# Two A/B transformer layers, forward and backward, on one core: gradient rows kept in SBUF, inner gradients turned through two small tiles, slope loads a group ahead

## The chip, the cores and the metric

The kernel runs on one core of one Trainium2 chip. It is written in Bass with the Tile framework: the program names tiles in pools, and the framework places them in SBUF or PSUM, orders each engine's instructions by a planner of its own and sets every semaphore. The metric is the device time of one execution in microseconds (us); lower is better.

## The reference

`x` has 2048 rows of D = 512, all in bf16. Four layers follow one another, A, B, A, B, each with a LayerNorm and a residual, and both A layers share their weights, as do both B layers. The kernel returns the output and, for a given `grad_out`, the gradients of `x` and of the five weights.

```python
def _A_ref(x, wqkv, wo):                       # linear attention, 32 heads of 16
    q, k, v = split(x @ wqkv)
    phi = lambda t: jnp.where(t > 0, t + 1, jnp.exp(t)) + 1e-6
    kv = einsum("bhsd,bhse->bhde", phi(k), v); z = phi(k).sum(over s)
    o = (phi(q) @ kv) / (phi(q) . z + 1e-6)
    return merge_heads(o) @ wo
def _B_ref(x, w_gate, w_up, w_down):           # GLU, F = 1376
    return (sigmoid(x @ w_gate) * (x @ w_up)) @ w_down
x = x + _A_ref(ln(x)); x = x + _B_ref(ln(x)); x = x + _A_ref(ln(x)); x = x + _B_ref(ln(x))
_out, _vjp = jax.vjp(_f, A_x, A_wqkv, A_wo, B_w_gate, B_w_up, B_w_down)
_grads = _vjp(grad_out)
```

The listing is shortened; `ln` is the LayerNorm without scale and shift.

## The kernel before

**Tiling.** A row tile is 128 rows; a block is four of them (512 rows), so there are four blocks. F is cut into eleven chunks of 128 (`NFC`), the last of which overlaps the one before it by 32 columns (`FDUP`). A step is one chunk `fc` of one block `b`.

**Stages.** The forward layers 0, 1 and 2 come first. The last GLU, layer 3, does forward and backward together (`b_both`): in each step `glu` makes the gate and up products of a chunk, four matmuls multiply `grad_out` turned (`gT3_t`) with the turned down weight (`wdT`), and `scale` multiplies the result into the pair of slopes, which gives the inner gradient `dd` of the chunk (in the tile `sd_t`). At step 1 or 2 of the next block, `down(b - 1)` makes the output rows and `dh_b(b - 1)` multiplies the inner gradients with the turned up and gate weights `wuT` and `wgT`, row tile by row tile, eleven matmuls each; `ln_bwd` then takes each row tile through the LayerNorm and adds the gradient rows (`gn_t`). Behind that come the backward of layer 2 (`a_bwd`), of layer 1 (`b_bwd`), of layer 0, and the weight gradients (`dw_cols`, `dw_rows`, `dw_small`).

**The fill.** The down weight's gradient of layer 3 (`Fill`, 176 matmuls) has no consumer before the end. It is given out in small portions between the matmuls of the backward layers. Its operands are the hidden rows, read turned from DRAM (`hf_t`), and the gradient rows (`gf_t`), which it loads itself, into the same pool as `hf_t`.

**Inner gradients in DRAM.** The weight gradients need `dd` with rows on the partitions. Block 0 is stored as it is and turned when it is read. Blocks 1 to 3 are turned on the spot: `turn_dd` turns each chunk with one DMA into a tile `nat_t` that collects four chunks (1024 KB), and when a set of columns is full, the tile is queued in `k.nats` and a later `flush_nat` stores it. Chunk 10 overlaps chunk 9 in that tile, so chunk 9 is turned after it.

**Queues.** SP issues the loads, the turning DMAs and most stores, POOL (`k.st`) the others. An instruction of a queue that waits holds up all behind it. The framework's planner decides the order; a DMA that is not ready in its plan is passed by others that are.

**Buffers.** `h_t` and `hT_t` have four buffers each and serve LayerNorm rows, gradient rows and their turned copies in all stages. `wuT` and `wgT` are allocated from the right end of SBUF when layer 2 has left it, and loaded turned at once (`load_b_bwd`, L438 and L439). PSUM has eight banks; in the forward stages `bank` takes them alternately from two tags of four.

**Slopes.** `b_bwd` reads the slopes of layer 1 in groups of three or four chunks into `sh_t`, two buffers, at the start of each group (L937, L938).

Of the kernel before, what the change touches and what calls it, by code (L numbers as in the profile page):

```python
# [16 lines left out]
D = 512  # L17
# [38 lines left out]
class K:  # L56
    spread_banks, n_bank = True, 0
# [13 lines left out]
def kernel(  # L71
# [72 lines left out]
    k.wb = ExitStack()  # L144
# [82 lines left out]
class Fill:  # L227


    def __init__(self, k):  # L230
        self.k, self.sv = k, k.sv[3]
        self.g = [k.p_set.tile([P, NB, D], BF16, name="gf_t", tag="set_t") for _ in range(NBLK)]
        for b in range(NBLK):
            k.nc.sync.dma_start(out=self.g[b][:], in_=by_tile(k.g_in, b * NB, NB))
        self.todo = self.run()
# [115 lines left out]
def forward(k):  # L351
    nc, tc = k.nc, k.tc
    with ExitStack() as ctx:
# [29 lines left out]
        for b, fc in b_both(k, 3, lns[3], ctx):  # L383
            if b == 0:
# [5 lines left out]
                if next(second, None) is None and actx:  # L390
                    flush_turned(k)
                    actx.close()
                    wb = w_pool(k, "wb")
                    k.wuT = wb.tile([P, NFC, D], BF16, name="wuT")
                    k.wgT = wb.tile([P, NFC, D], BF16, name="wgT")
                    load_b_bwd(k, k.wuT, "wu", k.last_mul)
                    load_b_bwd(k, k.wgT, "wg", k.last_mul)
                    actx = None
# [318 lines left out]
def last_grads(k, b):  # L717

    k.gns[b] = k.p_h.tile([P, NB, D], BF16, name="gn_t", tag="h_t")
    k.nc.sync.dma_start(out=k.gns[b][:], in_=by_tile(k.g_in, b * NB, NB))  # L720
    k.gTs[b] = k.p_hT.tile([P, NDC, SB], BF16, name="gT3_t", tag="hT_t")
    k.nc.sync.dma_start_transpose(out=k.gTs[b][:], in_=k.g_in[rows(b * NB, NB), :])


def b_both(k, l, ln, ctx):
# [4 lines left out]
    k.n_t, k.fused, k.early = 2, lambda st: True, []  # L730

    def down(b):
        for j in range(NB):
# [3 lines left out]
            if j % 2 == 0:  # L737
                ost = k.p_o.tile([P, 2, D], BF16, name="o0_t")
            nc.vector.tensor_tensor(ost[:, j % 2, :], y_ps[:], k.xs[st][:], ALU.add)
            if j % 2:  # L740
                k.st.dma_start(out=by_tile(k.out0, st - 1, 2), in_=ost[:])

    def scale(b, fc, dhh, dd):
        k.last_mul = nc.vector.tensor_tensor(dd, dhh[:].unsqueeze(1).to_broadcast([P, 2, SB]), dd, ALU.mult)  # L744
        if b:
            if fc == NFC - 2:
                return
            turn_dd(k, sv, b, fc, dd)
            if fc == NFC - 1:
                turn_dd(k, sv, b, fc - 1, dds[b][fc - 1])  # L750
# [4 lines left out]
    for b in range(NBLK):  # L755
        ln.need(b * NB + NB - 1)
        hhs[b], dds[b] = [], []
        if b == 1:
            k.p_ln, k.p_o, k.p_nat, k.p_wt = pool("ln3", 2), pool("o3", 2), pool("nat", 2), pool("wt", 1)
        for fc in range(NFC):  # L760
# [18 lines left out]
            if b in (1, 2) and fc in (6, 8, 10):  # L779
                turn_weight(k, fc // 2 - 3 + 3 * (b - 1))  # L780
            if b == 2 and fc == 5:
# [7 lines left out]
    flush_nat(k, k.st)  # L789
# [12 lines left out]
def turn_dd(k, sv, b, fc, dd):  # L802

    i, f = divmod(fc, 4)
    p0 = FDUP if fc == NFC - 1 else 0
    if f == 0:
        k.nat = k.p_nat.tile([P, 2, NB, D], BF16, name="nat_t")
    k.nc.sync.dma_start_transpose(
        out=k.nat[:, :, :, f * P - p0:(f + 1) * P - p0].rearrange("p a j f -> p (a j) f"),
        in_=dd.rearrange("p a s -> p (a s)"))  # L810
    if f == 1:
        flush_nat(k)
    if f == 3 or fc == NFC - 2:
        w = SETS[i][1]
        k.nats.append((sv["ddN"][b, i, :, :, :, 0:w], k.nat[:, :, :, 0:w]))
# [13 lines left out]
def dh_b(k, l, b, dds, h, up=None):  # L829
    for j in range(NB):  # L830
        st = b * NB + j
        dh_ps = k.bank([P, D], F32, name="dh_ps")
        for i in range(2 * NFC):
            a, fc = divmod(i, NFC)
            k.nc.tensor.matmul(dh_ps[:], lhsT=dds[fc][:, a, rows(j)], rhs=(k.wuT, k.wgT)[a][:, fc, :],  # L835
                               start=(i == 0), stop=(i == 2 * NFC - 1))
        ln_bwd(k, l, st, dh_ps[:], h[:, j, :], k.xs[st][:] if up is None else up[:, j, :])
# [5 lines left out]
def backward(k):  # L843
    nc, tc = k.nc, k.tc
    with ExitStack() as ctx:
        pool = lambda name, bufs, **kw: ctx.enter_context(tc.tile_pool(name=name, bufs=bufs, **kw))
        k.spread_banks = False
        mctx = ctx.enter_context(ExitStack())
        mpool = lambda name, bufs: mctx.enter_context(tc.tile_pool(name=name, bufs=bufs))
        k.p_set, k.p_sh = mpool("dw_set", 6), mpool("sh", 2)  # L850
# [11 lines left out]
        k.p_all = pool("dw_all", 2, side="right")  # L862
        a_bwd(k, 0, True)
        k.fill.step(NFC * NST)
        h3, h1 = (load_all(k, sv[l]["h"], k.p_all, "all", k.marks[b]) for l, b in ((3, 2), (1, 3)))
        joint = lambda i, a: dw_cols(k, ("wu", "wg")[a], 0, SETS[i],
                                     [(h3, sv[3]["ddT"][a], sv[3]["ddN"][:, :, :, a]), (h1, sv[1]["ddT"][a])])
        k.p_dst, k.n_put = mpool("dw_stage", 6), 0
# [3 lines left out]
        k.p_set = pool("dw_set_end", 12)  # L872
# [16 lines left out]
def ln_bwd(k, l, st, dh_ps, h_st, up):  # L889
# [9 lines left out]
    junk = k.p_ln.tile([P, D], BF16, name="junk", bufs=1)  # L899
    nc.vector.scalar_tensor_tensor(junk[:], t_sb[:], -1.0 / D, h_st, ALU.mult, ALU.mult, accum_out=c2[:])  # L900
# [8 lines left out]
def b_bwd(k, l):  # L909
    nc, sv = k.nc, k.sv[l]  # L910
    with ExitStack() as ctx:
# [21 lines left out]

        gTs[0], k.early = k.early, []
        for b in range(NBLK):
            for f0, nf in FGRP:
                sh = k.p_sh.tile([P, 4, 2, SB], BF16, name="sh_t", tag="sh")  # L937
                nc.sync.dma_start(out=sh[:, 0:nf].rearrange("p f a s -> p f (a s)"),  # L938
                                  in_=sv["sd"][:, b * NFC + f0:b * NFC + f0 + nf])
                for fc in range(f0, f0 + nf):  # L940
                    i = fc - f0
                    ps = k.bank([P, SB], F32, name="dhh_ps")
# [244 lines left out]
def dw_small(k):  # L1187
# [3 lines left out]
    for l in (2, 0):  # L1191
        sv = k.sv[l]
        C = k.p_set.tile([P, NDC, D], BF16, name="C_l", tag="set_t")
        nc.sync.dma_start_transpose(out=C[:], in_=sv["CT"][:])
        ET = k.p_set.tile([P, NDC, D], BF16, name="ET_l", tag="set_t")
# [19 lines left out]
def load_all(k, src, pool, tag, first=None):  # L1215
# [4 lines left out]
    else:  # L1220
        ts = [pool.tile([P, NB, D], BF16, name="rows_t", tag=tag)[:] for _ in range(NBLK)]
# [6 lines left out]

def pieces(k, nat, src, c0, w, turned=None):

    for b in range(NBLK):
        t = k.p_set.tile([P, NB, w], BF16, name="set_t", tag="set_t")
# [81 lines left out]
```

## Time and profile before

| What | Value |
|---|---|
| Median of 7 runs | 1109.94 us (1107.54 to 1113.09) |
| The profiled execution, its own time | 1111.71 us |
| Its span, first to last instruction | 1110.0 us |
| Granted TensorE clock | 0.996 |
| Busy time: PE, DVE, ACT, POOL | 1068.1, 552.3, 445.1, 301.1 us |
| DMA traffic | 260.07 MB, mean 234 GB/s |
| `nat_t<-sd_t` turning DMAs | 33, 4.1 us to landing |
| `sv_ddN<-nat_t` stores | 6 of 1024 KB and 3 of 704 KB |
| `gn_t` and `gf_t` loads | 4 and 4 of 512 KB |

How to read it: PE is TensorE's matmuls, PEld its weight loads, DVE VectorE, ACT ScalarE, POOL GpSimd, SP SyncE. A row of the groups names line, engine, operation, output and inputs, then busy time and mean duration, then the idle time before it and who ended it. Matmuls overlap in time, so a matmul's listed duration (379 ns) is longer than the distance to the next. The time of the profiled execution includes 1.7 us around its span.

### The profile page before, as it was taken

Reading aid. Unit: us, or ns where it says so; the run is one execution under the profiler, and the core shown is the slowest. Engines: PE = TensorE matmul, PEld = TensorE weight load, DVE = VectorE, ACT = ScalarE, POOL = GpSimd, SP = SyncE. Lnnn points to the kernel's source line nnn. Section 1 sums busy time; section 2 is a strip of 40 time slices with the busy share of each in tenths; the row PEclk is TensorE's granted clock in tenths of the full one; section 3 lists DMA queues with packets and bytes.
Section 4 is the critical chain, followed back from the end, with each engine's and each line's share of the span. In section 5 each row is a group of like instructions: output and inputs, shape, how many; then the busy total and the mean of one; then the engine's idle time right before and its main releaser. Section 6 shows DMA issues by size and latency. Waiting matters only on the chain.

```text
span 1110.0 us, 15238 instructions
## 1 busy us (share of the span) xinstructions
PE 1068.1 (96%) x5448; PEld 495.9 (45%) x5448; DVE 552.3 (50%) x1029; ACT 445.1 (40%) x930; POOL 301.1 (27%) x403
## 2 busy tenths in 40 slices
PE   6989899999989999999899999999999999999998
PEld 3444344444434444444344444443444444465443
DVE  7686865668834445444667535556876200001110
ACT  3476766548634646363234534433235200000010
POOL 5333534204631616141532200002623100011120
PEclk9999999999999999999999999999999999999999
DMA  8997977789994979899997897868989899599990
GB/s 249 257 254 246 282 213 231 217 196 230 301 212 106 268 183 266 212 248 264 319 333 211 222 282 226 237 190 232 350 235 339 225 248 203 123 212 229 258 233 29
DMA packets 387741, 260.07 MB, mean 234 GB/s; under 512 B 305424, under 2 KB 356400, under 8 KB 385616
## 3 DMA queue, kind: packets, MB, share of 16 engines
q1 hardware_dynamic: 372416, 208.98, 75.0%
q0 software_dynamic: 15248, 50.11, 13.6%
q8 instruction: 43, 0.70, 0.3%
q14 instruction: 34, 0.28, 0.1%
HBM read 77.76 MB, written 106.79 MB: 166 GB/s over the span
## 4 chain that ended last, share of the span: by engine, by line
PE 55%; DMA 2%; DVE 2%; ACT 2%; issue 1%; POOL 1%; SPq 0%; ACTq 0%; POOLq 0%; DVEq 0%
PE dw_ps L1258 18%; PE dh_ps L926 6%; PE dh_ps L1103 4%; PE dhh_ps L196 4%; PE dh_ps L835 3%; PE dw_ps L1276 3%; PE dh_ps L1094 2%; PE CT_ps L1022 2%; PE fill_ps L252 2%; PE y_ps L196 2%; PE dpk_ps L196 2%; PE dq_ps L196 2%; PE g_ps L196 1%; PE u_ps L196 1%; DMA qn_l<-sv_qn 1%
## 5 line engine op out<-in xcount | busy, mean ns | idle before, releaser
L1258 PE MATMUL dw_ps<-set_t,rows_t 128*128 128x512 bf16 (+1 forms) x1024 | 204.4, 362 | 0.0
L1258 PEld LDWEIGHTS <-rows_t 128*128 128x128 bf16 x1024 | 100.2, 98 | 103.6
L666 POOL TENSOR_TENSOR sd_t<-sd_t,hh_t 128x512 bf16<-128x512 bf16 x68 | 81.4, 1197 | 165.4 <-DVE hh_t L661 83.7
L1183 DVE CAST dw_new<-dw_ps 128x512 bf16<-128x512 f32 (+1 forms) x20 | 12.4, 654 | 185.4 <-PE dw_ps L1258 185.0
L1183 ACT CAST dw_new<-dw_ps 128x512 bf16<-128x512 f32 (+1 forms) x20 | 10.5, 561 | 225.7 <-PE dw_ps L1258 188.1
L896 ACT ACTIVATE t_sb<-dh_ps,rstd 128x512 f32<-128x512 f32 x64 | 43.5, 680 | 141.9 <-PE dh_ps L835 102.4
L196 PE MATMUL dhh_ps<-gT_t,wdT 128*128 128x512 bf16 x352 | 90.5, 379 | 1.8 <-ACT dhh_t L945 1.8
L196 PE MATMUL g_ps<-hT_t,wg 128*128 128x512 bf16 (+1 forms) x360 | 90.7, 374 | 1.3 <-DVE sd_t L663 0.6
L196 PE MATMUL u_ps<-hT_t,wu 128*128 128x512 bf16 (+1 forms) x360 | 90.7, 374 | 0.5 <-DVE hh_t L661 0.2
L926 PE MATMUL dh_ps<-wuT,dd_t 128*128 128x512 bf16 x176 | 66.7, 379 | 0.0
L926 PE MATMUL dh_ps<-wgT,dd_t 128*128 128x512 bf16 x176 | 66.7, 379 | 0.0
L661 DVE SCALAR_TENSOR_TENSOR hh_t<-sd_t,u_ps 128x512 bf16<-128x512 bf16 x88 | 59.4, 679 | 5.8 <-ACT sd_t L660 5.0
L660 ACT ACTIVATE sd_t<-g_ps,onef 128x512 bf16<-128x512 f32 x88 | 60.1, 691 | 2.5
L1184 POOL DMA_DIRECT2D out_dram<-dw_new x36 | 19.3, 541 | 154.2 <-DVE dw_new L1183 92.0
L947 DVE TENSOR_TENSOR dd_t<-dhh_t,sh_t 128x1024 bf16<-128x1024 bf16 x44 | 30.0, 691 | 59.9 <-ACT dhh_t L945 49.9
L835 PEld LDWEIGHTS <-sd_t 128*128 128x128 bf16 x352 | 34.8, 99 | 48.8 <-issue 8.7
L659 ACT ACTIVATE g_ps<-g_ps 128x512 f32<-128x512 f32 x88 | 52.4, 600 | 7.8 <-PE g_ps L196 7.4
L744 DVE TENSOR_TENSOR sd_t<-dhh_t,sd_t 128x1024 bf16<-128x1024 bf16 x44 | 30.4, 690 | 49.9 <-POOL sd_t L666 48.5
L196 PEld LDWEIGHTS <-wdT 128*128 128x128 bf16 x352 | 34.4, 98 | 43.5 <-issue 2.6
L196 PEld LDWEIGHTS <-wu 128*128 128x128 bf16 x360 | 35.2, 98 | 41.5 <-issue 0.7
L196 PEld LDWEIGHTS <-wg 128*128 128x128 bf16 x360 | 34.5, 98 | 42.0 <-issue 2.7
L926 PEld LDWEIGHTS <-dd_t 128*128 128x128 bf16 x352 | 34.4, 98 | 41.5
(166 smaller groups left out, 1841.9 us busy)
## 6 DMA issues: line engine op xcount, KB each, us to landing
sv_sd<-sd_t SPq DMA_DIRECT2D x22, 512.0 KB, 3.8
sv_ddT<-dd_t SPq DMA_DIRECT2D x40, 256.0 KB, 4.6
sv_h<-h_t POOLq DMA_DIRECT2D x16, 512.0 KB, 5.9
sv_qr<-pe_t POOLq DMA_DIRECT2D x16, 512.0 KB, 4.9
sh_t<-sv_sd SPq DMA_DIRECT2D x8, 1024.0 KB, 7.0
rows_t<-sv_h SPq DMA_DIRECT2D x16, 512.0 KB, 7.2
sv_ddN<-nat_t SPq DMA_DIRECT2D x6, 1024.0 KB, 6.0
set_t<-sv_ddN SPq DMA_DIRECT2D x12, 512.0 KB, 6.5
```

Source lines behind the costliest of these rows:

```text
L196: i = k.nc.tensor.matmul(out, lhsT=lhs(c), rhs=rhs(c), start=(c == 0), stop=(c == n - 1))
L659: nc.scalar.activation(g_ps[:], g_ps[:], ACT.Tanh, scale=-0.5)
L660: nc.scalar.activation(sd[:, 0, :], g_ps[:], ACT.Identity, bias=k.onef[:], scale=-1.0)
L661: nc.vector.scalar_tensor_tensor(hh[:], sd[:, 0, :], 0.5, u_ps[:], ALU.mult, ALU.mult)
L666: nc.gpsimd.tensor_tensor(sd[:, 1, :], sd[:, 1, :], hh[:], ALU.mult)
L744: k.last_mul = nc.vector.tensor_tensor(dd, dhh[:].unsqueeze(1).to_broadcast([P, 2, SB]), dd, ALU.mult)
L835: k.nc.tensor.matmul(dh_ps[:], lhsT=dds[fc][:, a, rows(j)], rhs=(k.wuT, k.wgT)[a][:, fc, :], start=(i == 0), stop=(i == 2 * NFC - 1))
L896: nc.scalar.activation(t_sb[:], dh_ps, ACT.Identity, scale=rstd, accum_out=c1[:])
L926: nc.tensor.matmul(acc[b][j][:], lhsT=dd[:, a, rows(j)], rhs=(k.wuT, k.wgT)[a][:, fc, :], start=(fc == 0 and a == 0), stop=(fc == NFC - 1 ...
L1103: nc.tensor.matmul(dh[j][:], lhsT=lhs(j, c), rhs=rhs(c), start=False, stop=stop and c == NDC - 1)
L1258: k.nc.tensor.matmul(ps[ic][:, 0:w], lhsT=h_m[:, ic * P:(ic + 1) * P], rhs=t_m, start=(m == 0), stop=(m == n - 1))
L1276: k.nc.tensor.matmul(p[0:r, :], lhsT=t[:, f:f + r], rhs=g_t, start=(i == 0 and st == 0), stop=(i == len(srcs) - 1 and st == NST - 1))
```

## The change

- The gradient rows of blocks 1 to 3 are loaded in their own block, at step 4, into a pool `gf` on the right side that lives to the end of the kernel; the fill uses them there. Those of block 0 still come early into `h_t` for `ln_bwd`, and once more at the end of `b_both` into the one-buffer pool `g0`, for the fill. At the end the hidden rows of layer 1 (`h1`) take these buffers.
- `turn_dd` collects two chunks instead of four, in a tile of 512 KB, alternately from a pool of its own and from `g0`, before that holds gradient rows. Every call first flushes what is queued. Chunk 10 has a tile of its own. The last flush goes to SP, not to POOL.
- `dh_b` of block 0 takes the four row tiles through `wuT` first and then through `wgT`, in four banks.
- `ln_bwd` in `b_both` writes an unused product to the PSUM bank it has read instead of to SBUF. `down` stores single row tiles.
- `b_bwd` loads each group of slopes one group ahead.
- In the tail, the pools for pieces, stages and rows are cut and placed anew: `dw_set` has two buffers and a right-side pool four, in turn.

```diff
@@ Fill
-        self.g = [k.p_set.tile([P, NB, D], BF16, name="gf_t", tag="set_t") for _ in range(NBLK)]
-        for b in range(NBLK):
-            k.nc.sync.dma_start(out=self.g[b][:], in_=by_tile(k.g_in, b * NB, NB))
+        self.g = k.gf
@@ forward, when layer 2 has left SBUF
+                    k.p_gf, k.p_g0 = gpool("gf", NBLK - 1), gpool("g0", 1)
                     wb = w_pool(k, "wb")
@@ last_grads
-    k.gns[b] = k.p_h.tile([P, NB, D], BF16, name="gn_t", tag="h_t")
-    k.nc.sync.dma_start(out=k.gns[b][:], in_=by_tile(k.g_in, b * NB, NB))
+    if b == 0:
+        k.gns[b] = k.p_h.tile([P, NB, D], BF16, name="gn_t", tag="h_t")
+        k.nc.sync.dma_start(out=k.gns[b][:], in_=by_tile(k.g_in, b * NB, NB))
...
+def rows_kept(k, b):
+    t = (k.p_gf if b else k.p_g0).tile([P, NB, D], BF16, name="gf_t", tag="gf_t")
+    k.nc.sync.dma_start(out=t[:], in_=by_tile(k.g_in, b * NB, NB))
+    return t
@@ b_both, down
-            if j % 2 == 0:
-                ost = k.p_o.tile([P, 2, D], BF16, name="o0_t")
-            nc.vector.tensor_tensor(ost[:, j % 2, :], y_ps[:], k.xs[st][:], ALU.add)
-            if j % 2:
-                k.st.dma_start(out=by_tile(k.out0, st - 1, 2), in_=ost[:])
+            ost = k.p_o.tile([P, D], BF16, name="o0_t")
+            nc.vector.tensor_tensor(ost[:], y_ps[:], k.xs[st][:], ALU.add)
+            k.st.dma_start(out=k.out0[rows(st), :], in_=ost[:])
@@ b_both, scale, loop and end
         if b:
-            if fc == NFC - 2:
-                return
             turn_dd(k, sv, b, fc, dd)
-            if fc == NFC - 1:
-                turn_dd(k, sv, b, fc - 1, dds[b][fc - 1])
...
+            if b and fc == 4:
+                gns[b] = rows_kept(k, b)
...
-    flush_nat(k, k.st)
+    flush_nat(k)
+    k.gf = [rows_kept(k, 0)] + [gns[b] for b in range(1, NBLK)]
     dh_b(k, l, b, dds[b], ln.h[b], gns[b])
@@ turn_dd
-    if f == 0:
-        k.nat = k.p_nat.tile([P, 2, NB, D], BF16, name="nat_t")
+    if f % 2 == 0:
+        k.n_nat = 1 - k.n_nat
+        k.nat = (k.p_g0, k.p_nat)[k.n_nat].tile([P, 2, NB, 2 * P], BF16, name="nat_t", tag=("gf_t", "nat_t")[k.n_nat])
...
-    if f == 1:
-        flush_nat(k)
-    if f == 3 or fc == NFC - 2:
-        w = SETS[i][1]
-        k.nats.append((sv["ddN"][b, i, :, :, :, 0:w], k.nat[:, :, :, 0:w]))
+    flush_nat(k)
+    if f % 2 or fc == NFC - 1:
+        p0, p1 = (0, 2 * P) if f % 2 else (FDUP, P)
+        c0 = f // 2 * 2 * P
+        k.nats.append((sv["ddN"][b, i, :, :, :, c0:c0 + p1 - p0], k.nat[:, :, :, p0:p1]))
@@ dh_b
+    dh = {}
+    for a, j in [(a, j) for a in range(2) for j in range(NB)] if b == 0 else [(a, j) for j in range(NB) for a in range(2)]:
+        if a == 0:
+            dh[j] = k.bank([P, D], F32, name="dh_ps")
+        for fc in range(NFC):
+            k.nc.tensor.matmul(dh[j][:], lhsT=dds[fc][:, a, rows(j)], rhs=(k.wuT, k.wgT)[a][:, fc, :],
+                               start=(a == fc == 0), stop=(a == 1 and fc == NFC - 1))
+        if a:
+            ln_bwd(k, l, b * NB + j, dh[j][:], h[:, j, :], up[:, j, :])
@@ ln_bwd
-    junk = k.p_ln.tile([P, D], BF16, name="junk", bufs=1)
+    junk = dh_ps if k.scrap_ps else k.p_ln.tile([P, D], BF16, name="junk", bufs=1)[:]
@@ b_bwd
+        groups = [(b, f0, nf) for b in range(NBLK) for f0, nf in FGRP]
+        shs = [slopes(*groups[0])]
...
+                sh = shs[-1]
                 for fc in range(f0, f0 + nf):
                     i = fc - f0
+                    if i == 1 and len(shs) < len(groups):
+                        shs.append(slopes(*groups[len(shs)]))
@@ backward, pools
-        k.p_set, k.p_sh = mpool("dw_set", 6), mpool("sh", 2)
+        k.p_set, k.p_sh = mpool("dw_set", 2), mpool("sh", 2)
...
-        k.p_all = pool("dw_all", 2, side="right")
+        k.p_all, p_first = pool("dw_all", 1, side="right"), pool("dw_first", 4, side="right")
...
+        h3 = load_all(k, sv[3]["h"], k.p_all, "all", k.marks[2])
+        h1 = load_all(k, sv[1]["h"], k.p_gf, "gf_t", k.marks[3])
+        k.set_pools = [p_first] * 4 + [k.p_set] * 2
...
-        k.p_dst, k.n_put = mpool("dw_stage", 6), 0
+        k.p_dst, k.n_put, k.n_set = pool("dw_stage", 6, side="right"), 0, -1
```

## The prediction

> **What bounds the kernel now.** I read the windows by stage first, because a mean over the whole span says nothing about the stage that an edit touches; then the waits of TensorE (PE), then the order of time around the two places that the diff moves.
>
> ```profile
> 337.00:490.00 153.00, 152.69 (x706) 68.89 (x705) 73.79 (x123) 89.11 (x180) 59.19 (x73) 1.00 0.86 209
> 515.50:545.00 29.50, 26.29 (x122) 11.65 (x120) 17.77 (x38) 12.20 (x24) 12.04 (x12) 1.00 1.00 262
> 630.00:755.00 125.00, 123.20 (x570) 55.63 (x569) 58.15 (x102) 48.17 (x107) 4.95 (x5) 1.00 0.80 225
> 860.00:1105.00 245.00, 245.00 (x1240) 120.20 (x1238) 26.16 (x43) 15.76 (x34) 29.57 (x51) 1.00 0.87 198
> ```
>
> First number after the stretch is its length, second PE's busy time. In the last GLU after its first block (337 to 490) PE misses 0.3 us, in the weight gradients (from 860) nothing. An edit there can only lose. What is left is in holes, and the waits name them:
>
> ```profile
> PE dh_ps L835 <- DMA wgT<-in_B_w_gate_dram: 4.2, 1, 4.2
> PE CT_ps L1022 <- DMA qn_l<-sv_qn: 2.7, 1, 2.7
> PE dhh_ps L196 <- ACT dhh_t L945: 1.8, 3, 1.0
> PE dh_ps L835 <- DMA wuT<-in_B_w_up_dram: 1.5, 1, 1.5
> ```
>
> The largest belongs to `dh_b` of block 0. In PE's order of time:
>
> ```profile
> 326.41 2.53 PE L835 MATMUL dh_ps<-wuT,sd_t 128*128 128x512 bf16 x11 [1.48 <-DMA wuT<-in_B_w_up_dram]
> 333.10 4.11 PE L835 MATMUL dh_ps<-wgT,sd_t 128*128 128x512 bf16 x11 [4.15 <-DMA wgT<-in_B_w_gate_dram]
> 337.00 2.69 PE L835 MATMUL dh_ps<-wuT,sd_t 128*128 128x512 bf16 x11
> 339.53 2.54 PE L835 MATMUL dh_ps<-wgT,sd_t 128*128 128x512 bf16 x11
> ```
>
> Eleven matmuls start 2.37 us apart as a group (339.53 to 341.90). PE does the eleven of wuT, then stands 4.15 us until wgT is there, and the eleven after it take 3.90 us (333.10 to 337.00) instead of 2.37: after the stop PE runs at half pace for a while. The DMA queue of SP says why wgT is late:
>
> ```profile
> 312.53 9.30 SPq L438 DMA_TRANSPOSE wuT<-in_B_w_up_dram  x1
> 321.88 1.27 SPq L439 DMA_TRANSPOSE wuT<-in_B_w_up_dram  x1
> 323.21 5.98 SPq L438 DMA_TRANSPOSE wgT<-in_B_w_gate_dram  x1
> 329.23 1.26 SPq L439 DMA_TRANSPOSE wgT<-in_B_w_gate_dram  x1
> ```
>
> The four transposes go out one behind the other; the last lands 4.1 us after 329.23, at 333.3.
>
> **Part 1: `dh_b` of block 0 goes by weight, not by row tile.** All four row tiles do wuT first. From 326.41 that is 44 matmuls, 4 x 2.37 = 9.5 us, so wgT is wanted at 335.9 instead of 328.8, and it is there at 333.3: 2.6 us to spare. Gone are the wait (4.15) and the half pace (3.90 - 2.37 = 1.5, and 0.15 in the next group): **-5.8 us**. The wait for wuT (1.48) stays; next after that nothing is late, as the GLU behind it has its inputs. The four `ln_bwd` now end 2.37 us apart; on DVE each costs 0.69 + 0.75 + 0.75 = 2.2 us, so DVE just keeps up and is at most about 1 us late for the next GLU, which PE runs ahead of by its banks. If wgT landed 2.6 us later than now, the gain would begin to shrink. Its new place in SBUF (16 KB lower, over the query tiles of layer 2) makes it wait for the stores of those; the last sv_qr store is issued at 299 and such stores take 4.9 us, and the sv_qn store for which wuT waits today ends later, at 312.5. So no delay.
>
> Of the two rules on the stop: the trace shows half pace after 4.15 us of waiting, and also after 2.40 us at 763.75, but not after 2.70 us at 543. The Trainium skill, "TensorE: Matmul & The Clock Gate", What's actually happening, puts the fall to half clock after an idle window of about 3.4 us. By the rule a new stop under 3.4 us would cost only itself, by the row at 763 it can cost 1.6 more; I price rivals by the row.
>
> **Part 2: gradient rows.** Loads of 512 KB fall from eight (gn x4, gf x4) to five. The three that go are 0.4 to 1.2 us of SP's queue each, between 490 and 502, where nothing waits for them: 0 on the path. The block's row load at fc 4 of its own block is wanted by `dh_b` more than 20 us later and lands in 5.0 to 6.5: hidden. The tag h_t loses three users, so the copies of `a_grads` 2, which today start at 517.88 when the h tile of block 3 frees, can go earlier, and their two transposes leave SP before 519. That takes some 4 us of SP work from ahead of the qn_l load whose lateness costs 2.7 us at 543. Between 0 and -2.7; I take 0, since SP's order there is the scheduler's and hf_t (6.0 us of SP) stays in front of it.
>
> **Part 3: two small tiles for the turned gradients.** The 33 transposes stay (4.1 us to land). The nine stores become 18: of 512 KB where they were 1024, in runs of 512 bytes. SP gets about 9 x 0.5 us more issue over 180 us. The waits are new. Each tile is refilled two pairs later: two transposes 2.6 us apart, 4.1 to land, the store 3.2 to 6.0 to land (wT 512 KB 3.2, the 1024 KB store 6.0), the issues 2: 12 to 15 us, against 4 x 2.59 = 10.4 us in which PE makes four more. So SP falls behind by 2 to 5 us per two pairs, and what is queued behind a blocked transpose waits too: weight turns and their stores (now written out at the next step, behind their own 8 us transpose), the transposes gT, hT, gaT. Against that stand margins: hT of block 2 lands about 7 us before PE asks, gT more, and each block has 28 us of `down` and `dh_b` in which SP catches up. The inner gradient tiles sd_t have a ring of 14 steps. Cost on the path in blocks 1 and 2: 0.
>
> In the last block there is no such gap. A rule speaks against the change here: the Trainium skill, "DMA: Bandwidth & Descriptors", Rules for kernel authors, wants 1 MiB or more per DMA, and its fit (Anatomy of one DMA[...]) is about 2.0 us fixed plus bytes over 436 GB/s: 3.2 us for half a store where the whole took 4.4. The trace's rows are 3.2 to 6.0 us. At the end the chain is: transpose of fc 10 waits for its tile, lands, its store lands, then the gradient rows of block 0 load into the same buffer, and the fill's first matmul needs them. SP today:
>
> ```profile
> 489.87 0.60 SPq L821 DMA_DIRECT2D sv_ddN<-nat_t  x1
> 499.93 1.23 SPq L808 DMA_TRANSPOSE nat_t<-sd_t  x1
> 501.97 3.14 SPq L240 DMA_TRANSPOSE hf_t<-sv_hhT  x1
> 505.48 0.34 SPq L1000 DMA_DIRECT2D MT_l<-wT  x1
> 507.10 5.75 SPq L240 DMA_TRANSPOSE hf_t<-sv_hhT  x1
> ```
>
> Stepping through the pairs of block 3 with 4 us per transpose and 5.5 per store I get the transpose of fc 10 at 499, landed 504, stored 509, rows there at 514. Today's fill starts at 515.35. By the page's 3.2 us it would be 507. If hf_t and MT_l are queued behind the row load, hf_t lands at 516.5, 1.2 us late. So this part costs 0 to 1.2, I take 0; with stores of 7 us, seen in this stretch, it costs 6 or more.
>
> **Part 4: small edits.** `down` stores each row tile alone: 8 more POOL issues of 0.73 us where POOL idles 2.5 to 4 us before each, and with two small tiles DVE waits about 1.7 us for the store before last (4.3 to 5.7 to land against 4.75); the 19 us of `dh_b` behind it cover that, else about 3 us per block. The squared-sum output goes to the PSUM bank: by the nearest rows 0.69 (as now) to 0.75 (a f32 output), 16 times, at most 1 us of DVE, hidden behind PE; the bank is held 1 us longer and eight banks cover it. Slope loads a group ahead: SP already issues them when a buffer frees (643.60 right after the product at 643.16), and PE's three waits there (1.8) name ACT, not sh_t: 0, bounds -1.8 and +0.5. Pools of the tail: PE is full from 800 on, the number of piece tiles is the same, the h1 rows load at 831 after the fill's last matmul at 806: 0. But four piece tiles are free from 755 rather than 787, so a turned piece (6 us of SP) may jump into the start of the last A backward: 0 to +4.
>
> **Sum.** -5.8 + 0 + 0 + 0 = -5.8 us on a profiled execution of 1111.7 (span 1110.0 and 1.7 around it), which is 1.8 above the median 1109.94. I subtract from the median: 1104.1, say 1104. About 0.3%, 3.3 us, is what a measurement of this kernel can tell from no change.
>
> **Rivals.** (a) The stop at wgT goes and the SP relief also ends the qn_l wait: -5.8 - 2.7 = -8.5, 1101.5. For it, two transposes leave the crowd; against it, hf_t stays. 0.2. (b) The stop goes, but a late fill or a jumping piece gives back 3 to 6 us: 1107 to 1110. 0.18. (c) The slower side: the two small tiles. If each store takes 9 us rather than 5.5, four stores in the chain of block 3 put the rows about 14 us later, at 528: PE stops 12.7 us at the start of the fill plus 1.6 at half pace, net +8.5, 1118.5. It decides from a store time near 8 us (net +3.3). For it: the queue took 6.7 us for a store there; against: three loads less in the same stretch. 0.14. (d) The order of `dh_b` does nothing because wgT comes later in the new layout: about 1110, within (b). The main case has 0.48, its own range 1102.5 to 1106.
>
> **Numbers.** Faster: main and (a), 0.68. Same: (b), 0.18. Slower: (c), 0.14. Range 1100 to 1112: below it part of (a), above it (c).
>
> **What would show it.** Right: no wait at L835 for wgT, 44 matmuls of wuT in a row near 326, PE's half pace gone there. Wrong in part 3: a PE wait at L252 for gf_t or hf_t at the start of the fill, SP waits at L808 for sv_ddN. Wrong in part 4: PE waits at L196 or L835 for o_t or t_sb, a set_t transpose between 755 and 785. The forecast fails if wgT lands over 2.6 us later, or if the new waits on SP reach PE.

## The result and the profile after

The changed kernel takes 1098.31 us (median of 12 runs, 1095.49 to 1104.15) against 1109.88 us of the kernel before on the same chip (31 runs). The ratio is 0.9902, 95% interval 0.9884 to 0.9919: 1.0% faster, about 11.6 us, twice the 5.8 us of the main case and just below the range (1100 to 1112). The profiled execution spans 1096.1 us at a granted TensorE clock of 0.997; the one shown of before spanned 1110.0.

The windows by stage, at the corresponding places of the new span (same columns as before: stretch, length, then busy time and count of PE, PEld, DVE, ACT, POOL, the granted clock, DMA share, GB/s):

```profile
337.00:482.00 145.00, 145.00 (x674) 65.59 (x672) 72.31 (x119) 87.52 (x176) 57.56 (x72) 1.00 0.99 223
507.66:537.00 29.34, 29.00 (x134) 12.97 (x133) 20.11 (x44) 10.95 (x21) 12.82 (x13) 1.00 1.01 296
622.00:747.00 125.00, 124.20 (x576) 56.15 (x575) 62.08 (x109) 49.59 (x113) 5.50 (x6) 1.00 0.78 222
852.00:1092.00 240.00, 240.00 (x1217) 117.94 (x1215) 21.03 (x35) 12.48 (x23) 28.36 (x51) 1.00 0.91 198
```

The last GLU and the weight gradients were full and stay full. The two stretches between them changed. Around the fill's start PE misses 0.3 us of 29.3, where it missed 3.2 of 29.5; in `b_bwd` 0.8 of 125, where it missed 1.8. Both count.

Four of PE's waits in the back part (engine, line, tile and what it waited for: us in total, times, longest):

```profile
PE fill_ps L250 <- DMA hf_t<-sv_hhT: 2.6, 1, 2.6
PE dhh_ps L196 <- ACT dhh_t L961: 0.8, 2, 0.5
PE fill_ps L250 <- DVE dkT_t L1131: 0.3, 1, 0.3
PE CT_ps L1038 <- DMA qn_l<-sv_qn: 0.2, 1, 0.2
```

The waits for wgT (4.2) and wuT (1.5) are gone, and so, without having been counted on, is that for qn_l (2.7, now 0.2). What is left is one fill step that waits for its hf_t behind 748 us. Before had it too: the wait of 2.40 us at 763.75 is put down to ACT in its profile, but the hf_t of that step landed at 763.70. (MT_l, qp_l, dqT_t and qn_l are loads of the first half of layer 2's backward, `a_bwd1`; haT_l, pkT_l and ha_l of its second half, `a_bwd2`, which makes dkT_t; gaT_t is a turned gradient copy of `a_grads`.)

`dh_b` of block 0 in PE's order of time (start, duration, engine, line, operation), and then its weights on SP's queue:

```profile
315.93 9.66 PE L196 MATMUL y_ps<-wd,hh_t 128*128 128x512 bf16 x44
325.43 9.66 PE L840 MATMUL dh_ps<-wuT,sd_t 128*128 128x512 bf16 x44
334.92 9.66 PE L840 MATMUL dh_ps<-wgT,sd_t 128*128 128x512 bf16 x44
```

```profile
311.47 6.00 SPq L438 DMA_TRANSPOSE wuT<-in_B_w_up_dram  x1
317.52 2.12 SPq L439 DMA_TRANSPOSE wuT<-in_B_w_up_dram  x1
319.69 6.88 SPq L438 DMA_TRANSPOSE wgT<-in_B_w_gate_dram  x1
326.61 1.26 SPq L439 DMA_TRANSPOSE wgT<-in_B_w_gate_dram  x1
```

The four transposes of the weights still leave one behind the other, until 327.9. But wgT, which landed at 330.8, is now wanted at 334.9; 88 matmuls run without a gap or a slow group.

SP at the end of the last GLU, where the prediction had stepped the chain of the two small tiles:

```profile
488.39 1.24 SPq L812 DMA_TRANSPOSE nat_t<-sd_t  x1
489.73 0.66 SPq L825 DMA_DIRECT2D sv_ddN<-nat_t  x1
490.44 5.16 SPq L995 DMA_TRANSPOSE gaT_t<-ga_t  x1
495.66 0.58 SPq L825 DMA_DIRECT2D sv_ddN<-nat_t  x1
496.36 2.49 SPq L238 DMA_TRANSPOSE hf_t<-sv_hhT  x1
499.15 0.40 SPq L728 DMA_DIRECT2D gf_t<-in_grad_out_dram  x1
```

The last transpose landed at 494.2, its store at 499.1, the row load behind it at 503.9; the fill starts at 507.66. That leaves 3.7 us. The page gives 4.5 us from issue to landing as the median of the 512 KB stores; the last two of 488 to 499 us took 7.5 and 3.5.

To see where the 11.6 us come from, I split PE's order of time at the same instructions in every traced kernel: the first matmul of `dh_b` of block 0, the first fill step, the first matmul of layer 1's `b_bwd`, the first dq_ps of layer 0, PE's last matmul. Each entry is a length in us.

| kernel | start to `dh_b`(0) | to fill | to `b_bwd` | to layer 0 | to the end | sum |
|---|---|---|---|---|---|---|
| before | 326.4 | 188.9 | 112.7 | 129.0 | 348.4 | 1105.5 |
| before, again | 323.9 | 187.2 | 113.1 | 129.5 | 348.9 | 1102.6 |
| new order alone | 323.5 | 182.9 | 112.9 | 128.5 | 346.9 | 1094.9 |
| changed | 325.4 | 182.2 | 108.7 | 127.8 | 348.6 | 1092.7 |
| changed, again | 325.0 | 182.2 | 109.1 | 128.0 | 347.4 | 1091.7 |
| changed, order undone | 325.1 | 189.0 | 108.3 | 127.9 | 349.0 | 1099.3 |

Between the means of the two traces of each, the change brings -5.8 us in the second column, -4.0 in the third, -1.3 in the fourth and -0.7 in the last: together 11.8, close to the 11.6 of the medians. The first column moves by 2.5 us and the last by 1.2 from one execution of the same program to the next.

Each row is one execution. The one of the new order alone was the fastest of its eight (1099.91 us, median 1105.17), so its sum flatters it by some 5 us. The medians below do not divide the gain as the table does: on one chip the order alone took 8.0 us off and the rest alone 9.2, together more than the whole 11.6, with intervals of some 4 to 11 us each.

### The profile page after: what moved, and what is told of

Same layout as the page of the kernel before. It is cut to its first block, busy times and chain, and to the rows that moved or that the text cites. A ratio compares the mean times of both kernels' runs of the same rounds, so it can differ in the third digit from the quotient of the medians.

```text
span 1096.1 us, 15266 instructions
## 1 busy us (share of the span) xinstructions
PE 1065.4 (97%) x5448; PEld 495.3 (45%) x5448; DVE 555.7 (51%) x1029; ACT 444.0 (41%) x930; POOL 302.7 (28%) x410
## 4 chain that ended last, share of the span: by engine, by line
PE 67%; DMA 2%; ACT 1%; DVE 1%; issue 1%; POOL 0%; SPq 0%; ACTq 0%; DVEq 0%; POOLq 0%
PE dw_ps L1280 19%; PE dh_ps L840 7%; PE dh_ps L934 7%; PE dhh_ps L196 6%; PE dh_ps L1119 4%; PE y_ps L196 4%; PE dw_ps L1298 3%; PE u_ps L196 3%; PE g_ps L196 3%; PE dh_ps L1110 3%; PE fill_ps L250 2%; PE CT_ps L1038 2%; PE dq_ps L196 2%; PE dpk_ps L196 2%; DMA hf_t<-sv_hhT 1%
```

## The experiments

**The order of `dh_b`.** The change without the new order, the order without the rest, and the kernel before once more.

```diff
# e1_order_undone, on the changed kernel
-    for a, j in [(a, j) for a in range(2) for j in range(NB)] if b == 0 else [(a, j) for j in range(NB) for a in range(2)]:
+    for a, j in [(a, j) for j in range(NB) for a in range(2)]:
# e2_order_alone, on the kernel before: dh_b(0) with the changed kernel's loop
# e7_before_again: no edit
```

> The changed kernel (1098.3 us) with one thing put back: dh_b of block 0 goes row tile by row tile again. Theory H (two holes: the stop at wgT, and the copies of a_grads that waited for an h_t buffer): in the changed kernel's trace PE reaches the first wuT matmul at 325.4, wgT lands at 330.8, and row by row it would be wanted 2.37 us after the first, at 327.8; so a stop of about 3.0 us and about 1.5 us of half pace come back: 1102 to 1104.5. Theory L (the new place in SBUF lets the two weights land early enough by itself, and the order does nothing): 1098, no wait for wgT at L840.

> The kernel before (1109.9 us) with the new order of dh_b of block 0 and nothing else. Theory H: the stop at wgT (4.15 us) and the half pace (1.6) go, the wait for wuT (1.5) stays if it belongs to the old placement, and nothing else moves: 1102.5 to 1104.5, and the qn_l hole of 2.7 us near 540 us is still there. If the wait for wuT varies from execution to execution, it may be absent here. Rival: with the new order the whole gain of 11.6 us comes, as the later holes were only echoes of the stop: 1098.

> The kernel before, unchanged, for a second trace: which of its holes recur. Theory H: the stop at wgT (about 4 us) and the qn_l hole (about 2.7 us) recur, as they follow from orders and buffers. The wait for wuT (1.5 us) recurs if it belongs to the old placement, and is between 0 and 3 us if it only follows how fast the queue moves in that execution. Time about 1110.

On one chip, where before took 1113.14 us: e1 1103.92 us, ratio 0.9925 (0.9899 to 0.9951); e2 1105.17 us, 0.9933 (0.9900 to 0.9967); e7 one time, 1107.72. PE's order of time, first e1, then e2:

```profile
325.14 2.53 PE L840 MATMUL dh_ps<-wuT,sd_t 128*128 128x512 bf16 x11
331.59 3.57 PE L840 MATMUL dh_ps<-wgT,sd_t 128*128 128x512 bf16 x8 [3.92 <-DMA wgT<-in_B_w_gate_dram]
```

```profile
323.51 9.66 PE L835 MATMUL dh_ps<-wuT,sd_t 128*128 128x512 bf16 x43
333.01 7.29 PE L835 MATMUL dh_ps<-wgT,sd_t 128*128 128x512 bf16 x32
```

(The window of the last line ends inside its group.) With the order undone the stop for wgT is back (3.9 us, and eight matmuls take 3.6 us, at half pace); with the order alone it is gone. In the table the order is worth 6.8 us from the one side (189.0 against 182.2) and 4.3 to 6.0 from the other (182.9 against 187.2 and 188.9). By the medians, e1 and the changed kernel (0.9902, 0.9884 to 0.9919) are not told apart, so what the order is worth within the full change rests on the traces. The wait for wuT, which the prediction let stand, is 1.5 us in one trace of before and absent in the other: it belongs to the execution, not to the kernel. The waits of e2 show what the order leaves:

```profile
PE CT_ps L1023 <- DMA qn_l<-sv_qn: 2.6, 1, 2.6
PE fill_ps L252 <- DMA hf_t<-sv_hhT: 2.5, 1, 2.5
```

The stop for the third qn_l is there in the three traces of before and of the order alone (2.7, 2.6, 2.6) and nearly gone in all with the rest of the change. So there is a second part of the gain, and it comes from the rest: e1, which has the rest without the order, is faster than before, with an interval that ends at 0.9951.

**The rows.** The change with the rows of blocks 1 to 3 for `ln_bwd` in h_t again, loaded a block ahead; the kept copies for the fill stay.

```diff
# e3_rows_in_h, last_grads
-    if b == 0:
-        k.gns[b] = k.p_h.tile([P, NB, D], BF16, name="gn_t", tag="h_t")
-        k.nc.sync.dma_start(out=k.gns[b][:], in_=by_tile(k.g_in, b * NB, NB))
+    k.gns[b] = k.p_h.tile([P, NB, D], BF16, name="gn_t", tag="h_t")
+    k.nc.sync.dma_start(out=k.gns[b][:], in_=by_tile(k.g_in, b * NB, NB))
# b_both: the kept tiles are a second copy, for the fill alone
-                gns[b] = rows_kept(k, b)
+                kept[b] = rows_kept(k, b)
...
```

> The changed kernel with the gradient rows that ln_bwd adds loaded into h_t again, a block ahead, as before; the kept copies for the fill are loaded too (three more loads of 512 KB, all before 345 us in the trace of after). Theory H: the copies of a_grads 2 wait for an h_t buffer until the end of dh_b of block 3 again, their two transposes come back behind it on SP, and the qn_l hole (about 2.9 us) returns: 1101 to 1103. Rival S (the hole went because the four gradient loads left SP's queue between 490 and 502 us): no change, 1098.

1107.06 us against 1113.14, ratio 0.9951 (0.9917 to 0.9984), an interval that just touches the changed kernel's. Part of the gain seems to be given back, but not where I looked. The trace (of an execution of 1101.88 us, among the quickest of nine) has no stop for qn_l, but 2.1 us at the fill step that waits for dkT_t at 573 us, and 3.0 us at the start of `b_bwd`. The four transposes of the last gradient copies are behind the fill's start again (511 to 519 us), and the third qn_l leaves SP 20.6 us after that start instead of 18.7; it landed in 4.3 us instead of 6.1, so it was there in time all the same. A theory of one stop was too narrow.

**The three loads that are gone.** The order alone with three of the fill's four row loads replaced by zeros from GpSimd (that gradient then leaves three blocks' rows out), and the reverse: the change with two of its kept blocks loaded a second time.

```diff
# e9_loads_off_sp, on e2
-            k.nc.sync.dma_start(out=self.g[b][:], in_=by_tile(k.g_in, b * NB, NB))
+            if b == 0:
+                k.nc.sync.dma_start(out=self.g[b][:], in_=by_tile(k.g_in, b * NB, NB))
+            else:
+                k.nc.gpsimd.memset(self.g[b][:], 0.0)
# e10_loads_on_sp, on the changed kernel, after the last flush_nat
+    for c in (1, 2):
+        held(k, k.last_mul, k.nc.sync.dma_start(out=gns[c][:], in_=by_tile(k.g_in, c * NB, NB)))
# e8_after_again: the changed kernel, no edit
```

> The kernel before with the new order at block 0's dh_b, and with three of the four row loads at the fill's start replaced by a fill with zeros from GpSimd: those three blocks' rows are left out of the down-projection's weight gradient, and SP has three loads less. Theory queue: the stop for the third qn_l comes from what SP has in hand around the fill's start; with three loads less the third qn_l leaves SP at least 1.5 us sooner after the fill's start than in the kernel with the order alone (22.2 us after it), and the stop (2.8 us there) is under 1 us. Rival, memory: it comes from the first dqT_t load, which waits 3.4 us after the fill's start for the last ln_bwd because it lies where the gradient rows lay; then the third qn_l leaves as late as before and the stop stays at 2.4 us or more.

> The changed kernel with two of its kept row blocks loaded a second time by SP at the end of the GLU, near where the kernel before loaded them. Theory queue: the third qn_l leaves SP later than 18.7 us after the fill's start (by 1 to 3 us) and the stop for it is 1 to 3 us; the fill's start itself has 3.7 us to spare and may lose up to 1. Total +1 to +4 us against the changed kernel. Rival, memory: the third qn_l as early as in the changed kernel, no stop over 0.5 us, total within 1 us.

> The changed kernel once more, unchanged. Theory: what it gained in its first trace is made of stops that every execution of before has (gate weight 2.9 to 4.3 us, third qn_l 2.8 us, both with a slower stretch behind) and of smaller ones that come and go; so the ratio is 0.988 to 0.992, no stop at the first dh_b, at most 0.5 us at the third qn_l, and the stop at the fill step for the tenth hf_t (2.8 us, at about 748) is there again. Rival: the absence of the qn_l stop was the luck of one execution: it is back with over 2 us.

On a chip where before took 1110.68 us: e9 1103.92, ratio 0.9925 (0.9900 to 0.9951), as good as the order alone; e10 1101.56, 0.9912 (0.9881 to 0.9943); e8 1097.85, 0.9893 (0.9862 to 0.9924). Without the loads the third qn_l left only 0.8 us sooner (21.4 us after the fill's start) and PE stopped 1.7 us for it, and 3.9 us later at dkT_t; from the fill to `b_bwd` e9 took 116.9 us. With two loads back, qn_l left at 18.8 and the stage took 108.6, as in the changed kernel. So the number of loads is not what makes qn_l late. The trace of e10 is 5 us longer than that of e8 for a reason ahead of the edit: a wait of 1.3 us for an hT_t at 308 and one of 3.9 us for wuT at 329, in a stretch where both kernels have the same instructions in the same order.

**What stands where in SP's list.** In before the first dqT_t left SP 3.4 us after the fill's start, because it waited for the last `ln_bwd`; in the changed kernel it leaves at once. The program's text for it is the same in both: so the scheduler or the new place in SBUF moved it; no run separates the two. SP of before, then of the changed kernel:

```profile
518.73 0.32 SPq L1012 DMA_DIRECT2D dqT_t<-sv_qr  x1
519.17 5.01 SPq L979 DMA_TRANSPOSE gaT_t<-ga_t  x2
524.25 0.56 SPq L1012 DMA_DIRECT2D dqT_t<-sv_qr  x1
524.93 4.22 SPq L979 DMA_TRANSPOSE gaT_t<-ga_t  x2
529.20 0.84 SPq L1017 DMA_DIRECT2D qn_l<-sv_qn  x1
...
531.09 6.01 SPq L240 DMA_TRANSPOSE hf_t<-sv_hhT  x1
537.20 0.53 SPq L1017 DMA_DIRECT2D qn_l<-sv_qn  x1
```

```profile
507.85 0.33 SPq L1028 DMA_DIRECT2D dqT_t<-sv_qr  x1
...
513.84 4.11 SPq L995 DMA_TRANSPOSE gaT_t<-ga_t  x1
518.05 0.53 SPq L1033 DMA_DIRECT2D qn_l<-sv_qn  x1
...
519.62 6.00 SPq L238 DMA_TRANSPOSE hf_t<-sv_hhT  x1
525.73 0.53 SPq L1099 DMA_DIRECT2D haT_l<-sv_hT  x1
526.35 0.43 SPq L1033 DMA_DIRECT2D qn_l<-sv_qn  x1
```

From the fill's start (515.35 and 507.66) to the third qn_l it is 21.8 and 18.7 us: two gaT transposes fewer stand in front. The hf_t transpose of 6.0 us is still there, and it no longer matters. A haT_l of layer 2 has also slipped in ahead. Three kernels put these places back one or two at a time:

```diff
# e11_dqT_late, on the changed kernel, a_bwd1 (k.last_x: the last instruction of ln_bwd)
-    loads(0)
+    first = loads(0)
     rows_n(0)
+    if l == 2:
+        held(k, k.last_x, first[1])
# e12_rows_in_h_dqT_late: the same on e3
# e13_ha_late, on the changed kernel, a_bwd2: the first haT_l, pkT_l, ha_l behind the copy that starts woT and wqkvT
+    if l == 2:
+        held(k, k.mark2, *k.first_ha)
```

> The changed kernel with the first dqT_t load made to wait for the last ln_bwd before the fill, as it waits in the kernel before. The third qn_l left SP 17.5 to 19.1 us after the fill's start in the changed kernels with the gradient copies early, 20.6 with the copies late and this load early, 21.4 to 22.5 in all that have both late. Theory, two causes that add: the load alone moves it by 1 to 2 us, to about 20, and the stop for the third qn_l becomes 1 to 2 us; total +1 to +3 us against the changed kernel (ratio to before about 0.992). Rival, the copies alone: it stays at 17.5 to 19.1 and the stop under 0.7 us.

> The changed kernel with both undone: the rows of blocks 1 to 3 for ln_bwd in h_t, a block ahead (so that the last gradient copies come behind the fill's start), and the first dqT_t load waiting for the last ln_bwd. Theory, two causes that add: the third qn_l leaves SP 21.4 to 22.5 us after the fill's start, the stop for it is 2 to 3 us with a slower stretch behind: about 4 us more than the changed kernel there, ratio about 0.993 to 0.995. Rival, the place in SBUF or something else of the change: the stop stays under 1 us.

> The changed kernel with the first group of a_bwd2's loads (haT_l, pkT_l, ha_l) held behind the copy that also starts the four weight loads, where SP's list of the kernel before has it; the gradient copies and the first dqT_t stay early. From the fill's start to b_bwd's first matmul the kernels took 108.3 to 109.1 us with copies and dqT_t early, 110.9 with the copies late, 114.3 with dqT_t late, 114.7 with both late, 112.7 to 113.1 before; in the last four kinds the first haT_l also stands behind the weight loads and the long hf_t transpose. Theory A, it is this place in SP's list that costs: 111 to 114.5 here, most of it at the fill step that waits for dkT_t (some 573 us into the span), +2 to +4 us in all. Theory B, it is the dqT_t load itself: 108.3 to 109.5, total within 1 us of the changed kernel.

| kernel | gaT, dqT_t, haT_l | fill to `b_bwd` | median, and of before | ratio |
|---|---|---|---|---|
| changed, again | early, early, early | 109.1 | 1097.85, 1110.68 | 0.9893 (0.9862 to 0.9924) |
| e3 | late, early, late | 110.9 | 1107.06, 1113.14 | 0.9951 (0.9917 to 0.9984) |
| e11 | early, late, late | 114.3 | 1102.52, 1111.22 | 0.9905 (0.9873 to 0.9936) |
| e12 | late, late, late | 114.7 | 1105.69, 1111.22 | 0.9969 (0.9937 to 1.0001) |
| e13 | early, early, late | 115.0 | 1099.47, 1110.61 | 0.9897 (0.9867 to 0.9926) |

None has the stop for qn_l back (under 0.4 us in each), so both theories of e11 and e12 missed its place. All four have a stop at the fill step that waits for dkT_t instead: 2.1, 3.2, 3.8 and 4.3 us, counted from one matmul to the next, where the changed kernel has 0.4 to 0.6. The waits of e13 between 560 and 580 us, then SP's queue of e13 and of the changed kernel just ahead of that:

```profile
DVE dph_t L1127 <- DMA pkT_l<-sv_pkT: 5.6, 2, 5.3
PE fill_ps L250 <- DVE dkT_t L1134: 4.2, 1, 4.2
```

```profile
554.93 11.47 SPq L238 DMA_TRANSPOSE hf_t<-sv_hhT  x1
566.50 0.52 SPq L1101 DMA_DIRECT2D haT_l<-sv_hT  x1
567.12 1.02 SPq L1103 DMA_DIRECT2D pkT_l<-sv_pkT  x1
```

```profile
554.67 8.62 SPq L238 DMA_TRANSPOSE hf_t<-sv_hhT  x1
563.39 0.52 SPq L1099 DMA_DIRECT2D haT_l<-sv_hT  x1
564.00 0.38 SPq L1101 DMA_DIRECT2D pkT_l<-sv_pkT  x1
```

An hf_t transpose holds SP for 11.5 us, the pkT_l behind it leaves 3.1 us later (the two fills start within 0.3 us of each other), DVE stands before it, and the product dkT_t that PE's fill step needs is queued on DVE behind that. This hf_t is the fill's fifth. In fifteen of the sixteen traces its hold goes with the number of SP's DMAs that were issued and not yet landed when it left, and PE's stop for dkT_t goes with the hold:

| under way on SP | hold of SP, us | stop of PE, us | traces |
|---|---|---|---|
| 3 | 7.1 to 7.8 | none | before again, e1, e2, e4, e10 |
| 4 | 8.5 to 9.7 | 0.3 to 1.9 | before, changed twice, e3, e5, e6 |
| 5 | 10.2 to 11.5 | 3.0 to 4.2 | e9, e11, e12, e13 |

(Stops by the profile's idle time.) Late loads alone do not bring it: before again and e2 have all three late and no such stop, but in them PE had already stood 2.6 us for qn_l. Nor do early ones keep it away: the sixteenth trace, e14 below, has all three early, a hold of 11.0 us with three under way, and a stop of 3.1. So the reading that SP's list in layer 2 has no slack, and that what is put late comes out as a stop for qn_l or as one for dkT_t, fits these traces but is argued, not shown. By the times, both put back (e12) costs 7.5 us against the changed kernel with one other edit on the same chip (e5 below, 1098.15), and the intervals do not meet. For dqT_t with haT_l (e11, +4.4 by the medians) and for haT_l alone (e13, +1.6 against e8 in another set of runs) they do: e13's profiled execution, at 1107.0 us, was the slowest of its six (from 1097.1), so its 4.2 us are not the usual case. How the 4 us divide between the three places stays open.

**Slopes a group ahead.** The slope loads at the start of their own group, as before.

```diff
# e5_slopes_undone, b_bwd
-                sh = shs[-1]
+                sh = slopes(b, f0, nf)
-                    if i == 1 and len(shs) < len(groups):
-                        shs.append(slopes(*groups[len(shs)]))
```

> The changed kernel with each group of slopes loaded at the start of its own group, as before. Theory: the loads leave when their buffer comes free, which the place in the order doesn't move: within 0.5 us of the changed kernel, stops at the start of b_bwd about 1.1 to 1.3 us as there. Rival: the 0.5 to 1.5 us that b_bwd's start took less than in the kernels before came from this: then it is 0.5 to 1.5 us slower and the stops there are 1.7 to 2.8 us.

1098.15 us against 1111.22, ratio 0.9897 (0.9868 to 0.9926), the changed kernel's; from `b_bwd` to layer 0 127.9 us, against 127.8 and 128.0. Putting the slope loads back changes nothing that shows, so the 1.3 us that this stage gains have another cause, which no kernel here isolates. They lie in PE's waits for ACT's dhh_t: 1.8 and 2.3 us in the traces of before, 0.8 and 1.0 in those of the changed kernel.

**The two small tiles.** Every store of a turned tile is issued a second time, into scratch.

```diff
# e4_stores_twice, flush_nat (four-dimensional tiles only)
         (eng or k.nc.sync).dma_start(out=dst, in_=t)
+        k.nc.sync.dma_start(out=k.twice[k.n_two][:, :, :, 0:w], in_=t)
```

> The changed kernel with every store of an inner gradients' tile issued a second time, into scratch, so that each of the two small tiles comes free only after about 9 us instead of 4.5. Theory: the chain of the two tiles has little room (its last tile gave the fill's start 3.7 us), so the fill starts 5 to 15 us late: +5 to +15 us, all of it at the fill's start. Rival: SP has room between the stores, and the second store lands beside the first (5.5 to 6 us): within 2 us of the changed kernel.

1118.63 us against 1111.22, ratio 1.0061 (1.0033 to 1.0089). The page's row of stores (us from issue to landing) and PE at the fill's start:

```profile
sv_ddN<-nat_t SPq DMA_DIRECT2D x15, 512.0 KB, 3.8
twice<-nat_t SPq DMA_DIRECT2D x15, 512.0 KB, 5.5
```

```profile
524.48 5.28 PE L251 MATMUL fill_ps<-gf_t,hf_t 128*128 128x512 bf16 x12 [16.49 <-DMA hf_t<-sv_hhT]
```

A tile is free about 6 us after its first store's issue (500.63 to 506.66 near the end) instead of 4.5, and SP issues each time another store of 0.7 to 1.6 us. The fill starts 16.7 us late, and by the medians the kernel is 20.5 us slower than e5 on the same chip: the theory's direction, beyond its 5 to 15. The second stores also take SP's time, so this is not the price of the hold alone. It is the prediction's slower rival, at a milder price for a store than it named: its 9 us were not needed.

**What is left at 748 us.** Two tries at the largest remaining stop: five fill steps more in `b_bwd`'s last block, and a third buffer for hf_t.

```diff
# e6_fill_moved, b_bwd
-                        k.fill.step(5 if b == 0 else 3)
+                        k.fill.step(5 if b == 0 else 5 if b == NBLK - 1 and fc < 2 else 4 if b == NBLK - 1 else 3)
# e14_third_set: room from one wd_part, one w_t and two (of three) ab_o buffers
-        k.p_set, k.p_sh = mpool("dw_set", 2), mpool("sh", 2)
+        k.p_set, k.p_sh = mpool("dw_set", 3), mpool("sh", 2)
```

> The changed kernel with five fill steps more in the last block of layer 1's b_bwd, so that the chunk of the fill whose hf_t came late is asked for in b_bwd. Theory: the largest stop left in the back part (2.8 us at about 748, and some 1.5 us of half pace behind it) goes: 3 to 4.5 us less than the changed kernel, ratio to before about 0.987. Rival: the fill steps that are missing later leave a wait of 0.9 us open there, or the next hf_t comes late in the same way: 0 to +1 us against the changed kernel.

> The changed kernel with a third buffer for the fill's hf_t tiles, so that each load may leave a chunk sooner; the room comes from one wd_part and one w_t buffer and two of three ab_o buffers. Theory: the hf_t transposes that hold SP for 8.6 to 11.5 us in layer 2 and the one that came 2.8 us late at about 748 were asked for only when one of two buffers came free; with a third the stop at 748 and the half pace behind it go: 3 to 4.5 us less than the changed kernel, ratio to before about 0.986. Rival: a single w_t or wd_part buffer opens a new wait on DVE or ACT, or the transposes are only held elsewhere on SP: 0 to +4 us.

In both the stop at 748 falls to 0.5 us. e6: 1096.51 us against e8's 1097.85 on the same chip, ratio to before 0.9873 (0.9849 to 0.9896); the intervals overlap, so it is not shown to be faster than the change, and a new wait of 1.1 us for a qn_l of layer 0 stands at 784, beside one of 1.5 us for dkT_t. e14: 1099.98 us, ratio 0.9897 (0.9873 to 0.9922): no gain; its waits show the other stop instead,

```profile
PE fill_ps L250 <- DVE dkT_t L1131: 3.1, 1, 3.1
```

behind an hf_t that holds SP for 11.0 us at 553, where the changed kernel's takes 8.6 at 555. Neither is a version that clearly beats the changed kernel.

## Why the prediction was right and wrong

**Part 1, the order: right, in mechanism and size.** Taken: -5.8. Measured: -5.8 between the stages, -4.3 to -6.0 by the order alone, +6.8 with the order undone. That two figures agree to a tenth is luck: the stop was 4.15 us in the trace that the prediction read and 2.69 in the other one of before. wgT had 4.1 us to spare, not 2.6. That the wait for wuT stays was wrong as stated: it comes (1.5, and up to 3.9 us in e10) and goes with the execution.

**Part 2, the rows: the step that failed, a term that was mis-sized.** It was put at 0, and the stage gave 4.0 us. The prediction named the mechanism (the gradient copies go earlier, two transposes leave SP ahead of qn_l), bounded it at -2.7 and took 0 "since SP's order there is the scheduler's and hf_t (6.0 us of SP) stays in front of it". hf_t did stay, at 6.00 us, and the gain came all the same: two gaT transposes fewer lay ahead of both, the third qn_l left 3.1 us sooner after the fill's start, and its stop fell from 2.7 to 0.2 us. The bound was short too. It was the one wait that the prediction drew from the profile, but the stage from the fill to `b_bwd` holds a second one that SP's lateness can feed, for dkT_t. The trace of before that the prediction read has it, the other one has not:

```profile
PE fill_ps L252 <- DVE dkT_t L1115: 1.3, 1, 1.3
```

In some executions a slower stretch behind a stop comes on top. Rival (a), 1101.5, had the right form, and too little for the same reason. That the places in SP's list cost time is shown by e12 (7.5 us, intervals apart). Which edit moved them, and how the 4.0 us divide, stays open: e12 brings its cost as a stop for dkT_t and not as the one for qn_l, and no kernel undoes the pools of the tail, the two small tiles or the single-row stores by themselves.

**Part 3, the small tiles: right at 0, and closer than it looked.** I had the last transpose at 499, its landing at 504, the store at 509, the rows at 514; they were 488, 494, 499 and 504 in a kernel that is 7.7 us ahead at that place, so 2 to 3 us sooner than stepped. The stores took 4.5 us in the median, not 5.5. Nor did they take 3.2: the fit that gives it (the Trainium skill, "DMA: Bandwidth & Descriptors", Anatomy of one DMA) is for DMAs issued by GpSimd, and these left on SP. One hf_t was put ahead of the row load, so the fear of hf_t behind it fell. Twice as many stores of half the size did not delay the fill; no run has the large tiles in the changed kernel, so what the size itself costs is not shown. The price of rival (c), 1118.5, met e4's 1118.63 by luck: 6 us of hold and the extra issues already turned the change into a loss. Its turning point was off by its own sum, which gives +4.4 at 8 us a store, not +3.3.

**Part 4, the small edits: 0 in sum.** DVE waits 21.2 us in five waits for the single-row stores, all hidden in the two traces of the changed kernel (in e6's PE waited 0.55 us once for such a store, by the profile). The squared-sum output in PSUM costs 0.70 us where it cost 0.69. Slopes: 0 by e5. The first turned piece left SP at 774.19 after 786.95, as much sooner as the whole kernel is at that place: no jump.

**Outside all parts:** 1.3 us at `b_bwd`, not explained beyond the wait for dhh_t; 0.7 in the last column, which is within what two executions of one program differ by; and some 0.7 us between the order alone and the full change within the last GLU.

## What to carry to other kernels

A wait that the profile names on a DMA queue's load is one sample of that queue's lateness: when a change takes work off the list ahead of it, price the stage to the end of its queue, not the one wait, and then ask where the next late load would stop. Where the framework orders the queue, a change of buffers can move loads that the diff never mentions, so read the order of the stage's loads before and after. And before a ring is halved, double its hold time once on purpose: a chain with 3.7 us of slack at its end turned a gain of 12 us into a loss of 7 when each tile was held 1.5 us longer and stored twice.

## What the runs showed of the hardware

A stop of PE of one length cost twice in one execution and once in the next. At the same fill step, the windows behind a stop of 2.64 us (the changed kernel) and of 2.63 us (the same, again), with the granted clock in the third column from the end:

```profile
751.30:754.30 3.00, 2.97 (x8) 1.14 (x9) 1.36 (x3) 0.15 (x1) 1.06 (x1) 0.54 1.11 268
```

```profile
751.30:754.30 3.00, 2.95 (x14) 1.39 (x15) 1.35 (x3) 0.72 (x2) 1.47 (x2) 1.00 1.10 264
```

Eight matmuls against fourteen in 3 us: some 1.3 us more or not, in two executions of one program. The Trainium skill, "TensorE: Matmul & The Clock Gate", What's actually happening, puts the fall to half clock after at least one idle window of about 3.4 us and calls the window free-running. A stop of 2.64 us (3.0 from one matmul's start to the next) cannot fill such a window, and here it cost the clock all the same, so the measurement decides against the rule as a lower bound. That the window runs free would explain why the same stop is caught once and missed once; no run here moves the phase alone, so this is argued and not shown.

A DMA transpose held SP for between 1.2 and 11.5 us in the trace of the changed kernel, and every load behind it waited that long. I had counted its SP time as a constant of the transfer. At one and the same place, the fill's fifth hf_t, it was 7.1 to 7.8 us with three of SP's DMAs under way, 8.5 to 9.7 with four and 10.2 to 11.5 with five, in fifteen traces; some gaT and gT transposes with nothing under way took 1.23. The count is not the whole of it: elsewhere in the changed kernel an hf_t with four under way took 4.4 us (at 756), and a gaT with three took 1.23 (at 750). What sets the hold is not shown.
